# Transposing DMAs for tokens and attention output, a reordered head and new planner constants in a two-layer attention and FFN kernel

## The chip, the cores and the metric

The kernel runs on one core of one Trainium2 chip. The metric is the device time of one execution in microseconds; a time of a kernel is the median over several runs. A core has five engines that each work through their own instruction stream in order: TensorE (PE in the profile, PEld its weight loads), VectorE (DVE), ScalarE (ACT), GpSimd (POOL) and SyncE (SP, which issues DMAs). They wait for each other through semaphores.

## The reference

Two equal layers over 2048 tokens of width 512, in bfloat16, with 32 heads of 16 channels and an FFN of width 1792:

```python
def _A_ref(x, wqkv, wo):
    qkv = (x @ wqkv).reshape(B, S, 3, H, Dh).transpose(2, 0, 3, 1, 4)
    q, k, v = qkv[0], qkv[1], qkv[2]
    scores = jnp.einsum("bhqd,bhkd->bhqk", q, k) * (Dh ** -0.5)
    p = softmax(scores)
    o = jnp.einsum("bhqk,bhkd->bhqd", p, v)
    return o.transpose(0, 2, 1, 3).reshape(B, S, D) @ wo

def _B_ref(x, w_gate, w_up, w_down):
    return (gelu(x @ w_gate) * (x @ w_up)) @ w_down

for layer in range(2):
    x = x + _A_ref(layernorm(x), A_wqkv, A_wo)
    x = x + _B_ref(layernorm(x), B_w_gate, B_w_up, B_w_down)
```

Both layers use the same weights. The score matrices have 2 x 32 x 2048 x 2048 elements, and each needs a row maximum and an exponential.

## The kernel before, in words

**Data.** All weights, the keys (`KT`), the values (`VP`) and the residual stream (`X`, float32, 16 tiles of 128 tokens) stay in SBUF. `XNT` holds the normalised tokens with channels on the partitions, as projections need them; `ATT` holds the attention output of a block of up to 512 queries, tokens on the partitions, and `ATTT` two transposed tiles of it for the output projection.

**Work units.** A unit is a block of queries (512, and at the end of the second layer 256 and 128) times a group of four heads; there are 80 units. Each goes through two phases. In phase 1 PE multiplies queries and keys into PSUM (L1724) and DVE reduces each 128x512 tile to row maxima (L1742, one or two tiles an instruction). The negated maxima, transposed into `MT`, are moved by four small DMAs into spare rows of `QT` (L1127), so that phase 2's matmul, which computes the scores transposed (L1594), subtracts them. ACT takes the exponential from PSUM to `SCR` (L1570, one or two tiles an instruction), and PE multiplies that with the values and a column of ones (L1618) into bank 7. ACT copies the result to `ACCS`, POOL takes the reciprocal of the sum (L1186) and multiplies into `ATT` (L1191).

**Folds.** DVE's share can be shifted to ACT: PE multiplies queries with the difference of two key blocks (`KD`, L1543), ACT writes its Relu to `SCR` (L1550), and one DVE instruction (L1737) adds that to the other block's scores and takes the maximum of both. Without a fold two tiles are reduced, with it one instruction does for two.

**Background work.** Between the score tiles the kernel puts projections, output projections, the FFN, layer norms and transposes, each a generator ("chain") that yields when it needs an engine. `ln_to_xnt` normalises up to four tiles into two buffers `XN` (on POOL for most, DVE and ACT at the head) and transposes each: `transpose_tile` issues four 128x128 PE transposes against an identity (L866) into a PSUM bank, and `evac` copies the bank to `XNT` or `ATTT` on ACT (L720) or DVE (L718). `outproj` does the same from `ATT` to `ATTT`, one tile ahead of the matmul with `WO` (L703).

**What sets the order.** All streams are written out on the host before launch. A planner keeps a clock for each engine, with a fixed duration for each kind of instruction, and at each step emits what fits; `_Sched` turns data dependences into semaphore waits. So what the chip runs is a fixed order for each engine. 21 constants (how far phase 1 may run ahead, when to fold, in which pieces background work goes, and so on) change every 16 pairs of score tiles, by the table `PLAN`. PE also runs filler matmuls on a zero weight (L1766) to keep its clock up.

**Head.** SP loads the tokens and weights. DVE makes the statistics of tiles 0 to 7 (L730, L732, L733), POOL the power of -1/2 (L735), DVE the normalised tile (L742); ACT does the same for tiles 8 to 15 (L838, L845). The first four tiles feed the projections of `QT` and `KT` (L703, cast to `SG`, then moved by DMA at L1010 and L940). ACT first copies the pattern of ones and zeros into `KT` for two head groups (L566).

Of the kernel before, what the change touches and what calls it, by code (L numbers as in the profile page):

```python
# [8 lines left out]
ALU = mybir.AluOpType  # L9
# [5 lines left out]
LN_EPS = 1e-5  # L15
# [138 lines left out]
]  # L154


# [1853 lines left out]
```

## Time and profile before

| | |
|---|---|
| median of 3 runs | 2487.87 us (2487.69 to 2489.23) |
| profiled execution, its own time | 2489.29 us |
| span of its instructions | 2487.6 us |
| busy PE, DVE, ACT, POOL | 2416.8, 2388.4, 2353.1, 811.5 us |
| granted TensorE clock | 0.999 |
| DMA moved | 25.67 MB, mean 10 GB/s |

Busy time is the union of an engine's instructions. A group row gives line, engine, operation, output and input, count, then busy us and mean ns of one, then the engine's idle time just before such instructions and what ended it. A stretch row gives for each engine the busy us within the stretch. Times are from the span's start.

### The profile page before, as it was taken

The page shows a single profiled execution, that of the slowest core. Times are in us where ns is not written, and L with a number is a line of the kernel's source. Part 1 is how long each engine was busy: PE and PEld are TensorE (multiplying, and loading weights), DVE is VectorE, ACT ScalarE, POOL GpSimd, SP SyncE. Part 2 cuts the span into 40 slices and gives each one's busy share as a digit, 9 for nine tenths or more (in the row PEclk, how much of TensorE's full clock was granted, in tenths as well). Part 3 has the DMA queues.
Part 4 walks back from the last instruction along what each step waited for, and adds up shares of the span by engine and source line. Part 5 has one row for each costly group of instructions (what it writes and reads, how often), then busy time and mean ns, then how long its engine had stood idle before and what let it go on. Part 6 is the DMA issues. An engine that isn't in the chain of part 4 may idle for free.

```text
span 2487.6 us, 69334 instructions
## 1 busy us (share of the span) xinstructions
PE 2416.8 (97%) x30182; PEld 1152.2 (46%) x30182; DVE 2388.4 (96%) x3168; ACT 2353.1 (95%) x3394; POOL 811.5 (33%) x1298
## 2 busy tenths in 40 slices
PE   8999999999999999999999999999999999999999
PEld 3444445434454444344433445434444344544655
DVE  8999999999999999999998999999999999999993
ACT  7999999999999999899988999999999999989987
POOL 4112125234442353421224041543116321244420
PEclk9999999999999999999999999999999999999999
DMA  3110000000000000000000000000000000000000
GB/s 94 48 57 6 4 9 2 6 2 2 6 2 6 2 2 6 2 10 11 11 10 1 9 15 4 6 2 6 11 2 6 2 8 6 3 3 11 4 4 10
DMA packets 28913, 25.67 MB, mean 10 GB/s; under 512 B 10944, under 2 KB 27584, under 8 KB 28608
## 3 DMA queue, kind: packets, MB, share of 16 engines
q1 hardware_dynamic: 28608, 21.24, 3.3%
q8 instruction: 236, 3.87, 0.6%
q14 instruction: 69, 0.57, 0.1%
HBM read 10.22 MB, written 2.10 MB: 5 GB/s over the span
## 4 chain that ended last, share of the span: by engine, by line
PE 45%; DVE 31%; ACT 23%; issue 1%; ACTq 0%
DVE PM L1742 29%; ACT SCR L1570 21%; PE PS L1724 14%; PE PS L703 12%; PE PS L1618 10%; PE PS L1594 4%; PE PS L1766 3%; DVE SCR L1737 2%; ACT SCR L1550 1%; PE PS L866 1%; PE PS L1543 0%; ACT SG L720 0%; ACT XNT L720 0%; ACT L1286 0%; ACT ACCS L1176 0%
## 5 line engine op out<-in xcount | busy, mean ns | idle before, releaser
L1742 DVE TENSOR_REDUCE PM<-PS 128x1 f32<-128x512 f32 (+1 forms) x2527 | 2203.8, 934 | 47.4 <-PE PS L1594 19.5
L1570 ACT ACTIVATE SCR<-PS 128x1024 bf16<-128x1024 f32 (+1 forms) x2652 | 2015.4, 871 | 46.9 <-PE PS L1594 32.9
L1724 PE MATMUL PS<-KT,QT 32*128 32x512 bf16 x3908 | 1021.0, 385 | 38.0 <-DVE PM L1742 21.1
L1594 PE MATMUL PS<-QT,KT 32*128 32x512 bf16 (+2 forms) x5120 | 929.5, 340 | 3.1 <-ACT SCR L1570 2.2
L1618 PE MATMUL PS<-VP,SCR 128*128 128x51 bf16 (+1 forms) x16384 | 802.5, 187 | 9.8 <-ACT SCR L1570 6.1
L1618 PEld LDWEIGHTS PS<-VP,SCR 128*128 128x128 bf16 x16384 | 571.3, 96 | 471.8 <-issue 398.2
L1724 PEld LDWEIGHTS PS<-KT,QT 32*128 32x128 bf16 x3908 | 243.8, 91 | 543.8 <-DVE PM L1742 317.3
L1766 PE MATMUL PS<-WV,ZER 128*128 128x240 bf16 x2198 | 408.8, 266 | 5.5 <-ACT SCR L1570 3.6
L1186 POOL TENSOR_TENSOR RL<-ACCS,CM 128x16 f32<-128x16 f32 (+2 forms) x71 | 182.4, 2569 | 449.5 <-ACT ACCS L1176 449.0
L1594 PEld LDWEIGHTS PS<-QT,KT 32*128 32x128 bf16 x5120 | 250.5, 91 | 71.2 <-ACT SCR L1570 41.5
L1766 PEld LDWEIGHTS PS<-WV,ZER 128*128 128x128 bf16 x2198 | 165.2, 96 | 56.1 <-issue 39.7
L1083 POOL TENSOR_TENSOR PM<-PM 128x16 f32<-128x16 f32 (+3 forms) x142 | 32.6, 230 | 426.4 <-DVE PM L1742 410.4
L1304 POOL TENSOR_TENSOR HT<-HT,AO 128x512 bf16<-128x512 bf16 x96 | 111.2, 1162 | 173.9 <-ACT AO L1302 173.8
L1341 POOL TENSOR_TENSOR KD<-KT 128x512 bf16<-128x512 bf16 x80 | 92.3, 1155 | 154.3 <-PE PS L1543 154.3
L703 PE MATMUL PS<-WD,HT 128*128 128x512 bf16 x448 | 131.3, 381 | 0.0
L703 PE MATMUL PS<-XNT,WU 128*128 128x512 bf16 (+2 forms) x504 | 131.1, 357 | 0.1
L1550 ACT ACTIVATE SCR<-PS 128x512 bf16<-128x512 f32 (+1 forms) x134 | 105.8, 790 | 22.3 <-PE PS L1543 20.7
L1737 DVE CUSTOM_DVE_ANT_0 SCR<-PS,SCR 128x512 bf16<-128x512 f32 x188 | 121.9, 686 | 3.2 <-PE PS L1594 0.7
L703 PE MATMUL PS<-XNT,WG 128*128 128x512 bf16 (+2 forms) x504 | 121.3, 358 | 1.7 <-ACT HT L1286 1.7
L1206 POOL TENSOR_TENSOR X<-X,AO 128x512 f32<-128x512 f32 x45 | 57.0, 1268 | 184.3 <-ACT AO L1204 184.3
L1286 ACT ACTIVATE HT<-PS 128x512 bf16<-128x512 f32 (+2 forms) x126 | 68.4, 550 | 31.6 <-PE PS L703 31.1
L1191 POOL TENSOR_TENSOR ATT<-ACCS,RL 128x256 bf16<-128x256 f32 (+2 forms) x78 | 41.8, 536 | 67.1 <-DVE RL L1184 61.5
(118 smaller groups left out, 1112.5 us busy)
## 6 DMA issues: line engine op xcount, KB each, us to landing
KT<-SG SPq DMA_DIRECT2D x64, 64.0 KB
QT<-MT SPq DMA_DIRECT2D x244, 1.0 KB
QT<-SG SPq DMA_DIRECT2D x56, 64.0 KB
out_dram<-AO SPq DMA_DIRECT2D x16, 128.0 KB, 1.7
WG<-in_B_w_gate_dram SPq DMA_DIRECT2D x4, 448.0 KB, 4.8
WU<-in_B_w_up_dram SPq DMA_DIRECT2D x4, 448.0 KB, 5.1
WD<-in_B_w_down_dram SPq DMA_DIRECT2D x4, 384.0 KB, 4.7
QT<-MT SPq DMA_DIRECT2D x68, 0.2 KB
```

The costliest lines, as they stand in the source:

```text
L703: ins = e.matmul(out_ap, lhsT=l, rhs=r_, start=(i == 0), stop=(i == n - 1))
L1186: emit("pool", lambda e: e.tensor_tensor(RL[:, s, 0:4 * nq], lsum, AP(CM1, 0, [[1, 128], [0, 4 * nq]]), op=ALU.pow), r=[("ACCS", s), ("CM1 ...
L1304: emit("pool", lambda e, ft=ft, o=o: e.tensor_tensor(HT[:, ft, c0:c0 + n], HT[:, ft, c0:c0 + n], AO[:, o, 0:n], op=ALU.mult), r=[("AO", o) ...
L1341: emit("pool", lambda e: e.tensor_tensor(KD[:, s, :], KT[:, g, ka * 512:(ka + 1) * 512], KT[:, g, kb * 512:(kb + 1) * 512], op=ALU.subtrac ...
L1550: emit("act", lambda e: e.activation(PT[:, s0:s0 + cnt, :], PS[:, bk:bk + cnt, :], ACTF.Relu), r=bks, w=[("PT", s0 + d) for d in range(cnt ...
L1570: emit("act", lambda e: e.activation(dst, src, ACTF.Exp, scale=DH ** -0.5), r=[BK[bk + i] for i in range(cnt)], w=[("PT", i) for i in slot ...
L1594: ins = e.matmul(bank(bk)[:, i * n:(i + 1) * n], lhsT=KT[32 * j:32 * j + 32, g, kt * 128:(kt + 1) * 128], rhs=QT[32 * j:32 * j + 32, s, 0: ...
L1618: ins = e.matmul(acc, lhsT=PT[:, slot, i * n + qt * 128:i * n + (qt + 1) * 128], rhs=AP(VP, (kt * H + 4 * g + j) * 17, [[NTT * H * 17, 128 ...
L1724: ins = e.matmul(bank(b), lhsT=QT[32 * j:32 * j + 32, s, qt * 128:(qt + 1) * 128], rhs=KT[32 * j:32 * j + 32, g, kb * 512:(kb + 1) * 512], ...
L1737: emit("dve", lambda e, i=i, b=b, sl=sl: e.tensor_tensor_reduce(PT[:, sl, :], bank(b), PT[:, sl, :], 1.0, -3.0e38, ALU.add, ALU.max, po[:, ...
L1742: emit("dve", lambda e: e.tensor_reduce(po, PS[:, bs[0]:bs[0] + cnt, :], axis=AX.X, op=ALU.max), r=bks, w=[("PM", sm) + h[1:] for h in hs] ...
L1766: return e.matmul(PS[:, b, NACC:512], lhsT=ZER[:, :], rhs=WV[:, 0, 0:512 - NACC], start=(b != 7), stop=(b != 7), skip_group_check=True)
```

## The change

1. *Transposing DMAs.* Where a layer norm's tile goes to `XNT` and where a tile of `ATT` goes to `ATTT`, SP issues one `dma_start_transpose` of 128x512 instead of four PE transposes and an evacuation. Kept on PE: the first layer's tokens at the head, the last tiles of the first layer (its last attention block, its last FFN group and the tokens of the next layer that come from it), and the end of the second layer. The planner reckons 2.0 us of SP and 1.6 + 0.7 us until the tile has landed. There are four new DMA groups, alternating by tile; a DMA of a group waits for the one before it.
2. *Head.* Planner durations for the loads, for POOL's `KT` fills and a start at 0.6 us are set anew; loads no longer queue behind each other in its clock. ACT fills one block of `KT` for two groups, POOL the other three. Tile 3's mean and variance come from ACT (`ln_a3`); tiles 2 and 3 are normalised into `ATT` so that they need not wait for the transposes of 0 and 1; the evacuations of tiles 0 to 2 and the first query projection go to ACT. The 14 filler matmuls before the first score are dropped.
3. *Constants.* 109 of the 132 rows of `PLAN` differ, so the whole order of the streams does.

```diff
+        if grp is not None and self.groups[grp] and o.idx:
+            need((grp, o.idx - 1))
...
-        ... LM1=0, N0=14):
+        ... LM1=0, T0=0.6, A3=1, DTX=2, DTA=2, T_TP=0.7, T_TPI=2.0, VL=0):
...
+        tp_groups = ["tx0", "tx1", "ty0", "ty1"] if DTX or DTA else []
...
-                clk[eng] = start + T_DMA * nd
+                clk[eng] = start + (T_TPI if grp[0] == "t" else T_DMA * nd)
                 done = max(clk["dma"], clk[eng] + 1.6) + dur
-                clk["dma"] = done - 1.6
+                clk["dma"] = done - carry
...
-            emit(eng, lambda e: e.dma_start(dst, src), r=r, w=w, grp=grp, dur=mb * 5.0)
+            emit(eng, lambda e: e.dma_start(dst, src), r=r, w=w, grp=grp, dur=mb * 2.9, carry=0.0)
...
         for g in range(NFE):
-            kt_fill(g, "act")
+            kt_fill(g, "act", 0, 1 if A3 else NKB)
...
+        def ln_a3(tt):
+            c = [ACCS[:, 1, 40 + j:41 + j] for j in range(5)]
+            yield ("act", [XSK[tt]], [("X", tt)])
+            emit("act", lambda e: e.activation(X[:, tt, :], XS[tt], ACTF.Copy, accum_out=c[0]), ...)
+            yield ("pool", [("A3",)], [("A3",)])
+            emit("pool", lambda e: e.tensor_scalar(c[1], c[0], -1.0 / D, None, op0=ALU.mult), ...)
+            yield ("act", [("A3",)], [("AH", 3)])
+            emit("act", lambda e: e.activation(ATT[:, 3, :], XS[tt], ACTF.Square, bias=c[1], accum_out=c[2]), ...)
+            yield ("pool", [("A3",)], [("A3",)])
+            emit("pool", lambda e: e.tensor_scalar(c[3], c[2], 1.0 / D, LN_EPS, op0=ALU.mult, op1=ALU.add), ...)
+            emit("pool", lambda e: e.tensor_tensor(c[4], c[3], CM05[:, 0:1], op=ALU.pow), ...)
...
+        def dma_tile(src, rkeys, dst, wkeys, grp):
+            emit("sp", lambda e: e.dma_start_transpose(dst, src), r=list(rkeys), w=list(wkeys), grp=grp, dur=T_TP)
...
             for i, tt in enumerate(tts):
+                xs, sk = xn_slot(i, A3 and tag == ("in", 0) and tts[0] == 0)
                 yield ("cond", lambda i=i: at["xn"] >= i)
+                if DTX and tag != ("in", 0) and not fast and (DTX == 1 or tag not in (("mid", 0), ("in", 1)) or tts[-1] * 128 + 128 < S):
+                    yield ("sp", [sk], [("XNT", tt)])
+                    dma_tile(xs, [sk], XNT[:, :, tt * 128:(tt + 1) * 128], [("XNT", tt)], "tx%d" % (i % 2))
+                    ...
+                    continue
...
+            te = "sp" if DTA and not lastb and (DTA == 1 or la or t0 + n < S) else "pe"
             def tr(qt):
+                if te == "sp":
+                    dma_tile(ATT[:, qt, :], ak, ATTT[:, qt % 2, :, :], [("ATTT", qt % 2)], "ty%d" % (qt % 2))
+                else:
+                    transpose_tile(...)
...
-            if not pos["g"]:
-                for _ in range(N0):
-                    sch.op("pe", warm_fn(7), r=[("ZER",), ("WV",)], w=[BK[7]])
```

More of the change, by code (lines that the diff above doesn't have):

```diff
@@ L387, in _build @@
             sch.add_dma_group(g, serial=True)
-        dma_groups += out_groups + move_groups
+        tp_groups = ["tx0", "tx1", "ty0", "ty1"] if DTX or DTA else []
+        for g in tp_groups:
+            sch.add_dma_group(g, serial=True)
+        dma_groups += out_groups + move_groups + tp_groups
         for o in range(2):
@@ L396, in _build @@
         clk = {e: 0.0 for e in ("pe", "act", "dve", "pool", "sp", "dma")}
+        for e in clk:
+            clk[e] = T0
         rgf = [0.0] * 4
@@ L567, in kt_fill @@
                 KT[:, g, b0 * 512:b1 * 512].rearrange("p (a b) -> p a b", b=512), AP(HT, 0, [[NFT * ft_tok, 128], [0, b1 - b0], [1, 512]])),
-                r=[("HT", 0)], w=[("KT", g, b) for b in range(b0, b1)], dur=0.05 + 0.438 * (b1 - b0) if eng == "act" else 0.74 * (b1 - b0))
-            if b1 == NKB:
-                filled.add(g)
+                r=[("HT", 0)], w=[("KT", g, b) for b in range(b0, b1)], dur=0.05 + 0.438 * (b1 - b0) if eng == "act" else 0.08 + 0.48 * (b1 - b0))
+            filled.update((g, b) for b in range(b0, b1))
         N_FILL = NFA
         for g in range(NFE):
-            kt_fill(g, "act")
+            kt_fill(g, "act", 0, 1 if A3 else NKB)
         xn_late = [0]
         def fills_act():
+            if A3:
+                yield ("cond", lambda: xnt_rec.get(3) == ("in", 0))
+                for b in range(1, NKB):
+                    for g in range(NFE):
+                        yield ("pool", [("HT", 0)], [("KT", g, b)])
+                        kt_fill(g, "pool", b, b + 1)
             yield ("cond", lambda: kt_rec.get((0, NKB - 1)) == 0)
@@ L590, in fills @@
             for tt in range(8):
+                if A3 and tt == 3:
+                    continue
                 yield ("pool", [XSK[tt]], [("X", tt)])
@@ L722, in _build, with xn_slot, ln_fast @@
         ln_cnt = {"n": 0}
-        def ln_fast(tts, x_of, ready, at, dx=0.6):
+        sch.add_alias(("A3",), ("ACCS", 1))
+        def ln_a3(tt):
+            c = [ACCS[:, 1, 40 + j:41 + j] for j in range(5)]
+            yield ("act", [XSK[tt]], [("X", tt)])
+            emit("act", lambda e: e.activation(X[:, tt, :], XS[tt], ACTF.Copy, accum_out=c[0]),
+                 r=[XSK[tt]], w=[("X", tt), ("A3",)], dur=0.62)
+            yield ("pool", [("A3",)], [("A3",)])
+            emit("pool", lambda e: e.tensor_scalar(c[1], c[0], -1.0 / D, None, op0=ALU.mult), r=[("A3",)], w=[("A3",)], dur=0.24)
+            yield ("act", [("A3",)], [("AH", 3)])
+            emit("act", lambda e: e.activation(ATT[:, 3, :], XS[tt], ACTF.Square, bias=c[1], accum_out=c[2]),
+                 r=[XSK[tt], ("A3",)], w=[("AH", 3), ("A3",)], dur=0.7)
+            yield ("pool", [("A3",)], [("A3",)])
+            emit("pool", lambda e: e.tensor_scalar(c[3], c[2], 1.0 / D, LN_EPS, op0=ALU.mult, op1=ALU.add), r=[("A3",)], w=[("A3",)], dur=0.24)
+            emit("pool", lambda e: e.tensor_tensor(c[4], c[3], CM05[:, 0:1], op=ALU.pow), r=[("A3",), ("CM05",)], w=[("A3",)], dur=0.59)
+            a3["done"] = True
+        a3 = {}
+        def xn_slot(i, head):
+            return (ATT[:, i - 2, :], ("AH", i - 2)) if head and i >= 2 else (XN[:, i % 2, :], ("XN", i % 2))
+        def ln_fast(tts, x_of, ready, at, dx=0.6, late=None):
+            head = late is not None
             for i in range(len(tts) + 1):
-                if i < len(tts):
+                if i < len(tts) and tts[i] != late:
                     xa, xk = x_of(tts[i])
@@ L739, in ln_fast @@
                     xa, xk = x_of(tts[k])
-                    yield ("cond", lambda k=k: at["tr"] > k - 2)
-                    yield ("dve", [xk, ("LNR", k)], [("XN", k % 2)])
-                    emit("dve", lambda e, k=k, xa=xa: e.tensor_scalar(
-                        XN[:, k % 2, :], xa, MV[:, k, 0:1], LNS[:, 1, k:k + 1], op0=ALU.subtract, op1=ALU.mult),
-                        r=[xk, ("MV", k), ("LNR", k)], w=[("XN", k % 2)], dur=dx)
+                    xs, sk = xn_slot(k, head)
+                    yield ("cond", lambda k=k: head or at["tr"] > k - 2)
+                    if tts[k] == late:
+                        yield ("cond", lambda: "done" in a3)
+                        yield ("dve", [xk, ("A3",)], [sk])
+                        emit("dve", lambda e, xa=xa, xs=xs: e.tensor_scalar(
+                            xs, xa, ACCS[:, 1, 41:42], ACCS[:, 1, 44:45], op0=ALU.add, op1=ALU.mult),
+                            r=[xk, ("A3",)], w=[sk], dur=dx)
+                        at["xn"] = k
+                        continue
+                    yield ("dve", [xk, ("LNR", k)], [sk])
+                    emit("dve", lambda e, k=k, xa=xa, xs=xs: e.tensor_scalar(
+                        xs, xa, MV[:, k, 0:1], LNS[:, 1, k:k + 1], op0=ALU.subtract, op1=ALU.mult),
+                        r=[xk, ("MV", k), ("LNR", k)], w=[sk], dur=dx)
                     at["xn"] = k
@@ L892, in ln_to_xnt @@
             if tag == ("in", 0):
-                add(ln_fast(tts, x_of, ready, at, 0.3), due)
+                if A3 and tts[0] == 0:
+                    add(ln_a3(3), due)
+                add(ln_fast(tts, x_of, ready, at, 0.3, 3 if A3 and tts[0] == 0 else None), due)
             else:
@@ L930, in kproj @@
                 yield ("cond", lambda: last_u in p2_done)
-            yield ("cond", lambda: 2 * c in filled and 2 * c + 1 in filled)
+            yield ("cond", lambda: (2 * c, b) in filled and (2 * c + 1, b) in filled)
             yield ("cond", lambda: all(xnt_rec.get(4 * b + i) == ("in", la) for i in range(4)))
@@ L946, in vproj @@
         def vproj(la, tt):
+            if not la and VL:
+                yield ("cond", lambda: kt_rec.get((0, NKB - 1)) == 0)
             if la:
@@ L998, in qproj @@
             yield ("cond", lambda: all(xnt_rec.get(tt) == ("in", la) for tt in tts))
-            s = yield from proj(WQ, "WQ", g // 2, t0, n, tts)
+            s = yield from proj(WQ, "WQ", g // 2, t0, n, tts, "act" if A3 and u == 0 else None)
             for i in range(2):
@@ L1217, in outproj @@
             nq = n // 128
+            te = "sp" if DTA and not lastb and (DTA == 1 or la or t0 + n < S) else "pe"
             def tr(qt):
[L1219 to L1220 removed]
+                if te == "sp":
+                    dma_tile(ATT[:, qt, :], ak, ATTT[:, qt % 2, :, :], [("ATTT", qt % 2)], "ty%d" % (qt % 2))
+                else:
+                    transpose_tile(lambda ck: ATT[:, qt, ck * 128:(ck + 1) * 128], ak, ATTT[:, qt % 2, :, :],
+                                   [("ATTT", qt % 2)])
                 if qt == nq - 1:
                     att_free["bi"] = bi
[L1224 removed]
+            yield (te, ak, [("ATTT", 0)])
             tr(0)
@@ L1229, in outproj @@
                 if qt + 1 < nq:
-                    yield ("pe", ak, [("ATTT", 1 - s)])
+                    yield (te, ak, [("ATTT", 1 - s)])
                     tr(qt + 1)
```

32 lines of the change are left out of this document (17 added, 15 removed), and 210 rows, old and new, of the table PLAN.

## The prediction

> **What bounds the kernel now.** I read the page first: engine shares, the 40 slices, the chain that ended last.
>
> ```profile
> span 2487.6 us, 69334 instructions
> PE 2416.8 (97%) x30182; PEld 1152.2 (46%) x30182; DVE 2388.4 (96%) x3168; ACT 2353.1 (95%) x3394; POOL 811.5 (33%) x1298
> ...
> DVE  8999999999999999999998999999999999999993
> ACT  7999999999999999899988999999999999989987
> ...
> DVE PM L1742 29%; ACT SCR L1570 21%; PE PS L1724 14%; PE PS L703 12%; PE PS L1618 10%; PE PS L1594 4%; PE PS L1766 3%; DVE SCR L1737 2%; ACT SCR L1550 1%; PE PS L866 1%; PE PS L1543 0%; ACT SG L720 0%; ACT XNT L720 0%; ACT L1286 0%; ACT ACCS L1176 0%
> ```
>
> DVE (row maxima) and ACT (exponentials) are both full nearly everywhere; PE's 97% includes filler matmuls (L1766), so it is not the limit by itself. The transposes and their evacuations have about 1% of the chain (PE L866), so they count through the engine time that they take, not as links. Then the stretch view, for where DVE still idles:
>
> ```profile
> 450.00:475.00 25.00, 24.43 (x340) 12.63 (x340) 24.82 (x35) 24.96 (x29) 5.85 (x12) 1.00 0.01 2
> ...
> 1350.00:1375.00 25.00, 24.68 (x262) 10.51 (x260) 21.20 (x30) 21.10 (x31) 10.28 (x17) 1.00 0.01 1
> ...
> 2425.00:2450.00 25.00, 24.95 (x462) 15.43 (x457) 12.27 (x25) 24.54 (x36) 0.88 (x3) 1.00 0.01 3
> 2450.00:2475.00 25.00, 24.58 (x366) 14.14 (x365) 6.24 (x15) 19.49 (x26) 1.62 (x5) 1.00 0.05 17
> ```
>
> The columns after the length are busy PE, PEld, DVE, ACT, POOL. In mid layer DVE has 24.8 of 25 us, ACT as much. At the layer seam both drop (21.2). In the tail DVE is done and ACT, with PE, sets the end. So a change is worth what it takes off DVE up to its last reduction, plus what it takes off ACT and PE behind that, plus the head.
>
> **DVE's work.** Each count below is the difference between the built instruction streams of the two kernels; each duration is of this trace.
>
> ```profile
> L1742 DVE TENSOR_REDUCE PM<-PS 128x2 f32<-128x1024 f32 x1193 | 1443.6, 1217 | 30.2 <-PE PS L1594 14.0 <-PE PS L1724 6.0 <-PE PS L1543 0.4
> L1742 DVE TENSOR_REDUCE PM<-PS 128x1 f32<-128x512 f32 x1334 | 895.9, 681 | 17.2 <-PE PS L1594 5.5 <-PE PS L1724 5.3
> L1737 DVE CUSTOM_DVE_ANT_0 SCR<-PS,SCR 128x512 bf16<-128x512 f32 x188 | 121.9, 686 | 3.2 <-PE PS L1594 0.7 <-PE PS L1724 0.6
> L1737 DVE DVE_READ_ACCUMULATOR2_ANT PM<- 128x1 f32 x188 | 15.6, 83 | 0.0
> L1296 DVE TENSOR_TENSOR HT<-PS,HT 128x512 bf16<-128x512 f32 x2 | 1.4, 686 | 0.0
> ```
>
> The new constants fold 14 more score tiles (a fold lets ACT take a Relu of a difference, so that one DVE pass serves two tiles). Folds: +14 x (0.686 + 0.083) = +10.8 us. Double reductions fall by 8: -8 x 1.217 = -9.7. Single ones fall by 12: -12 x 0.681 = -8.2. Five more products go into HT on DVE: +5 x 0.686 = +3.4. Two additions into X and a handful of small head forms leave it: about -3.8 (estimate, at 0.2 to 0.7 us each). Sum: **-7.5 us**. DVE did almost no transposition evacuations, so the DMA transposes give it nothing directly; its gain comes through the folds that ACT's freed time pays for.
>
> **ACT's work.**
>
> ```profile
> L1570 ACT ACTIVATE SCR<-PS 128x1024 bf16<-128x1024 f32 x1444 | 1382.5, 1074 | 31.1 <-PE PS L1594 23.4 <-PE PS L1724 0.7
> L1570 ACT ACTIVATE SCR<-PS 128x512 bf16<-128x512 f32 x1208 | 668.4, 629 | 15.7 <-PE PS L1594 9.5
> L1302 ACT ACTIVATE AO<-PS 128x512 f32<-128x512 f32 x96 | 59.2, 617 | 1.9 <-POOL HT L1304 1.1 <-PE PS L703 0.3
> ...
> L1550 ACT ACTIVATE SCR<-PS 128x1024 bf16<-128x1024 f32 x54 | 57.7, 1069 | 2.4 <-PE PS L1543 2.4
> L1550 ACT ACTIVATE SCR<-PS 128x512 bf16<-128x512 f32 x80 | 48.1, 601 | 19.9 <-PE PS L1543 18.3 <-PE PS L1724 1.1
> L720 ACT ACTIVATE XNT<-PS 128x512 bf16<-128x512 bf16 x61 | 38.6, 644 | 3.6 <-PE PS L866 3.4
> ...
> L720 ACT ACTIVATE ATTT<-PS 128x512 bf16<-128x512 bf16 x31 | 20.0, 648 | 2.1 <-PE PS L866 2.1
> ```
>
> The stream has 39 DMA transposes into XNT and 27 into ATTT; ACT loses 39 x 0.644 + 26 x 0.648 = -42.0 us of evacuations. It gains the folds' Relus, 4 x 0.601 + 5 x 1.069 = +7.7, and pays for a split that the new constants choose: 74 double exponentials become 148 single ones, 148 x 0.629 - 74 x 1.074 = +13.6. Three fewer AO copies: -1.9. KT fills given to POOL against the third tile's statistics taken over: about 0. Sum: **-22.6 us**, three times DVE's.
>
> **PE's work.**
>
> ```profile
> L1766 PE MATMUL PS<-WV,ZER 128*128 128x240 bf16 x2198 | 408.8, 266 | 5.5 <-ACT SCR L1570 3.6 <-ACT ACCS L1176 1.0 <-DVE PM L1742 0.3
> ...
> L866 PE MATMUL PS<-IDN,XN 128*128 128x128 bf16 x224 | 22.8, 226 | 9.2 <-DVE XN L742 9.2
> L866 PE MATMUL PS<-IDN,ATT 128*128 128x128 bf16 x160 | 15.3, 220 | 0.2 <-ACT AO L1204 0.2
> ```
>
> 264 of the 384 transposes go: 264 x (22.8 + 15.3)/384 = -26 us. 86 more fillers come: 86 x 408.8/2198 = +16. PE is relieved by 10 us that were not the limit; I count nothing for it.
>
> **Head.**
>
> ```profile
> 10.13 0.41 DVE L742 TENSOR_SCALAR XN<-SCR,MV,LNS 128x512 bf16<-128x512 bf16 x1
> 12.19 1.91 PE L703 MATMUL PS<-XNT,WQ 128*128 128x512 bf16 x4
> 17.05 0.69 DVE L718 CAST SG<-PS 128x512 bf16<-128x512 f32 x1 [0.89 <-PE PS L703]
> 20.96 0.38 PE L1724 MATMUL PS<-KT,QT 32*128 32x512 bf16 x1
> 21.39 0.69 DVE L1742 TENSOR_REDUCE PM<-PS 128x1 f32<-128x512 f32 x1 [0.97 <-PE PS L1724]
> ```
>
> The first projection waits for four normalised tiles; the fourth is written at 10.13. ACT now makes that tile's mean and square, which takes a statistics chain out of DVE's line and drops the six fillers that stood ahead of the projection. But ACT's two passes, its first evacuation and three POOL steps still follow each other, so I give it 1.0 us, between 0 and 2. The 14 fillers before the first score at 20.96 cost nothing now (the score waits for KT's move, issued after the cast at 17.05), so dropping them gives nothing. Head: **-1.0 us**.
>
> **Tail.**
>
> ```profile
> 2430.18 1.79 DVE L1742 TENSOR_REDUCE PM<-PS 128x2 f32<-128x1024 f32 x2
> ```
>
> Behind the last reduction (2431.97) the span runs 55.6 us more. Behind the last score matmul the old stream holds 304 quarter-tile phase-2 matmuls, the new one 276: 7 tiles of exponentials fewer, 7 x 1.074/2 = -3.8 us of ACT. Four more FFN matmuls stand there, at most +1.5 us of PE by the row of 0.38 us a score matmul. I take **-2.5**, between -3.8 and 0.
>
> **The DMAs.** What the trace does not show is a transposing DMA. Nearest rows, the last number being issue to landing in us, and the queue's waits:
>
> ```profile
> out_dram<-AO SPq DMA_DIRECT2D x16, 128.0 KB, 1.7
> ...
> HT<-in_A_x_dram SPq DMA_DIRECT2D x2, 512.0 KB, 8.6
> ```
>
> ```profile
> SPq L1127 <- DVE MT L1087: 1228.1, 54, 53.0
> ```
>
> A tile is 128 KB, so from release to landing I bound it by 1.7 and 8.6 us, and take 4: above the row of the same bytes, since it is cut finer. Does that hide? In the FFN a block is transposed between its last out-projection matmul and its first gate matmul, and the stream holds 20 to 91 phase-1 score tiles there. For third and fourth out-projection tiles 10 to 15 score tiles (0.61 us each by the double reduction) lie between the buffer's release and its reader: 6.1 to 9.2 us of cover. The least covered are 12 readers: the first out-projection tile of eight blocks and four V projections at the seam, placed where the planner expects the tile, 4.3 us after its source (its constants 2.0 + 1.6 + 0.7). If a tile is later, PE stands in order and all scores behind it; DVE and ACT run on for about a banked pair each, 1.2 us. Queued behind a transpose on SP are the next units' MT-to-QT moves, but SP waits 1228.1/54 = 23 us for each of those, and phase 2 runs 58 tiles or more behind, 35 us. POOL now waits for DMAs before reusing XN; it is 33% busy. So at 4 us the price is zero.
>
> The Trainium skill speaks against the swap: VectorE: DVE Perf Modes, in The three transpose paths, gives 1309 ns for a 128x128 block by DMA against 390 ns on TensorE, and its rules prefer TensorE where PSUM will do. By that figure a tile of four blocks would take 4 x 1309 ns = 5.2 us and, with half a microsecond to issue it, end at 5.7 (an estimate): 12 x 0.2 = 2 us of stalls, and a sum of -9. No trace here shows a transposing DMA yet.
>
> **Sum.** -7.5 - 1.0 - 2.5 = -11.0 us. The profiled execution took 2489.29 us around its span of 2487.6; it lies 1.4 us above the runs' median of 2487.87. 2487.87 - 11.0 = **2476.9, so 2477**.
>
> **Rivals.**
>
> *Both engines cash in (2465).* ACT gives 15 us more than DVE. If that also shortens DVE's waits (47.4 us stand before its reductions in the rows above, mostly after PE phase-2 matmuls that share PE's order with ACT's banks), a quarter of them is another -12. For: both engines are saturated in mid layer. Against: freed ACT time was spent on splitting exponentials, a sign of slack there.
>
> *It turns into idle time (2487).* New constants also move the seam, where DVE lost 3.8 us in 1350 to 1375 alone; 10 us more idling over the two seam stretches and the mid layers eats the sum. The planner's own durations are not the chip's, so a fresh plan may fit worse.
>
> *Slower: late tiles (2489 to 2514).* If a tile lands later than 4.3 + 1.2 = 5.5 us after its source, each of the 12 least covered readers stalls by the excess. The sum is gone at 12 x (L - 5.5) = 11, L = 6.4 us; at the upper bound of 8.6 the price is 12 x 3.1 = +37, so 2514. For: the upper row, and four tiles in a row on one queue. Against: that row moves four times the bytes.
>
> *Not done as told:* excluded, the stream holds the 66 transposes.
>
> **Numbers.** 0.2%, 5 us, is about what a measurement of this kernel can tell from no change. Chances: forecast 0.57, both cash in 0.17 (together faster, 0.74); idle time 0.12 (same); late tiles 0.14 (slower). The forecast's own bounds (head 0 to -2, tail 0 to -3.8) give 2475 to 2480. The range runs from 2462, a little under the first rival, to 2493, where L is 6.8: below lie some 0.06, above some 0.11.
>
> **What would show it.** Right: DVE busy near 2381 and ACT near 2330, the L720 XNT and ATTT groups at 22 and 5; first reduction near 20.4; last reduction to end near 53 us; PE waits on the transposes' queue near zero. Wrong: PE matmuls on ATTT or XNT led by DMA waits of over a microsecond; DVE idle above 107 us, above all in 1000 to 1425; a landing above 6.4 us.

## The result, and the profile after

The changed kernel takes 2481.66 us (median of 9 runs, 2480.65 to 2481.82), the kernel before 2488.09 us beside it (9 runs, 2487.44 to 2490.97). The ratio is 0.997, with an interval of 0.996 to 0.998: faster by 6.4 us. The profiled execution took 2481.77 us, around a span of 2480.0; its span is 7.6 us shorter than the one of before, whose profiled execution lay 1.2 us above its median while this one lies at its own.

From the page of the changed kernel, span, engine shares, two rows of the slices and the chain that ended last:

```profile
span 2480.0 us, 69071 instructions
PE 2409.1 (97%) x30004; PEld 1147.4 (46%) x30004; DVE 2382.1 (96%) x3173; ACT 2331.1 (94%) x3415; POOL 810.2 (33%) x1311
...
DVE  8999999999999999999998999999999999999993
ACT  7999998999989999899989999989999999978987
...
DVE PM L1806 31%; ACT SCR L1637 17%; PE PS L1791 16%; PE PS L717 13%; PE PS L1685 10%; PE PS L1661 4%; PE PS L1830 4%; DVE SCR L1801 1%; ACT SCR L1617 1%; PE PS L1610 0%; PE PS L914 0%; ACT AO L1266 0%; ACT ACCS L1238 0%; ACT L1637 0%; DVE ST L769 0%
```

ACT lost 22.0 us of work, DVE 6.3, PE 7.7. On the chain ACT's exponentials went from 21% to 17%, DVE's maxima from 29% to 31%, and the PE transposes (L914 now) from 1% to nothing. The groups (reductions L1806, folds L1801 with their Relus L1617, exponentials L1637, evacuations L736, fillers L1830):

```profile
L1806 DVE TENSOR_REDUCE PM<-PS 128x2 f32<-128x1024 f32 x1185 | 1433.6, 1218 | 35.2 <-PE PS L1661 18.1 <-PE PS L1791 5.9 <-PE PS L1610 0.2
L1637 ACT ACTIVATE SCR<-PS 128x1024 bf16<-128x1024 f32 x1370 | 1297.9, 1074 | 20.6 <-PE PS L1661 14.7
L1806 DVE TENSOR_REDUCE PM<-PS 128x1 f32<-128x512 f32 x1322 | 887.5, 681 | 12.3 <-PE PS L1661 7.1 <-PE PS L1791 1.3
L1637 ACT ACTIVATE SCR<-PS 128x512 bf16<-128x512 f32 x1356 | 726.6, 619 | 25.3 <-PE PS L1661 17.5
...
L1801 DVE CUSTOM_DVE_ANT_0 SCR<-PS,SCR 128x512 bf16<-128x512 f32 x202 | 130.1, 686 | 3.2 <-PE PS L1661 1.2 <-PE PS L1791 0.6 <-PE PS L1610 0.2
...
L736 ACT ACTIVATE XNT<-PS 128x512 bf16<-128x512 bf16 x19 | 11.4, 619 | 4.0 <-PE PS L914 4.0
...
L736 ACT ACTIVATE ATTT<-PS 128x512 bf16<-128x512 bf16 x5 | 3.0, 608 | 2.1 <-PE PS L914 2.1
```

The transposing DMAs, in the list of DMA issues (last number: median us from issue to landing), and in the waits (us in total, times, longest) the only engine that ever waited for one:

```profile
XNT<-XN SPq DMA_TRANSPOSE x39, 2.4
ATTT<-ATT SPq DMA_TRANSPOSE x27, 2.5
```

```profile
POOL XN L838 <- DMA XNT<-XN: 9.8, 3, 4.1
```

PE has no wait on them at all. Where the 7.6 us of span went is seen by cutting both spans at the start of the first reduction and at the end of the last. The columns after the length are busy PE, PEld, DVE, ACT, POOL; before first, then after:

```profile
0.00:21.39 21.39, 12.62 (x70) 7.07 (x71) 14.71 (x41) 15.76 (x33) 7.67 (x26) 1.00 0.62 190
21.39:2431.97 2410.58, 2351.91 (x29284) 1112.49 (x29282) 2358.04 (x3085) 2296.57 (x3301) 801.61 (x1266) 1.00 0.03 9
2431.97:2487.60 55.63, 52.27 (x831) 32.65 (x829) 15.60 (x44) 40.72 (x63) 2.21 (x7) 1.00 0.04 11
```

```profile
0.00:20.16 20.16, 11.27 (x57) 5.32 (x58) 13.67 (x37) 13.27 (x32) 10.02 (x31) 1.00 0.65 202
20.16:2426.86 2406.70, 2347.76 (x29181) 1110.78 (x29178) 2352.45 (x3094) 2279.84 (x3323) 797.99 (x1274) 1.00 0.05 12
2426.86:2480.00 53.14, 50.08 (x771) 31.32 (x769) 15.94 (x45) 37.95 (x62) 2.19 (x7) 1.00 0.04 12
```

Head -1.2, middle -3.9, tail -2.5. In the middle DVE has 5.6 us less work (2358.04 to 2352.45), but it idles 1.7 us more (2410.58 - 2358.04 = 52.5 before, 54.3 after). That extra idling has a place, 2200 to 2400 us, the second layer's small blocks; before, then after:

```profile
1000.00:1450.00 450.00, 437.41 (x5140) 198.30 (x5140) 425.34 (x563) 418.47 (x595) 127.67 (x181) 1.00 0.04 8
...
2200.00:2400.00 200.00, 196.73 (x3040) 105.89 (x3038) 196.06 (x249) 185.53 (x284) 85.39 (x170) 1.00 0.03 6
```

```profile
1000.00:1450.00 450.00, 441.50 (x5297) 202.17 (x5296) 428.81 (x555) 428.34 (x645) 139.22 (x187) 1.00 0.04 9
...
2200.00:2400.00 200.00, 193.19 (x3176) 108.35 (x3175) 191.33 (x244) 190.66 (x306) 78.88 (x161) 1.00 0.04 10
```

DVE's idle time there goes from 3.9 to 8.7 us, while ACT has 5 us more to do. Between 1000 and 1450 us it falls by 3.5.

Not all of that is the change. In the profiled execution of before, TensorE's granted clock (the column after POOL) fell once, to half for 3.4 us from 1409 us on. e10 below has the order of before behind the head, and in its profiled execution the clock stays at 1.0. The same stretch, before and in e10:

```profile
1400.00:1425.00 25.00, 24.09 (x319) 12.35 (x316) 23.27 (x35) 23.52 (x30) 2.42 (x5) 0.93 0.01 2
```

```profile
1400.00:1425.00 25.00, 24.12 (x339) 12.43 (x337) 24.48 (x37) 24.66 (x31) 2.41 (x5) 1.00 0.01 2
```

The reductions behind it come 1.3 us earlier in e10, beyond the lead that e10 had ahead of it. So about 1.3 us of the middle's 3.9 is this fall, about as much as that execution stood above its median (1.2).

### The profile page after: what moved, and what is told of

Its sections match the earlier page's. It is cut to its first block, busy times and chain, and to the rows that moved or that the text cites. A ratio compares the mean times of both kernels' runs of the same rounds, so it can differ in the third digit from the quotient of the medians.

```text
span 2480.0 us, 69071 instructions
## 1 busy us (share of the span) xinstructions
PE 2409.1 (97%) x30004; PEld 1147.4 (46%) x30004; DVE 2382.1 (96%) x3173; ACT 2331.1 (94%) x3415; POOL 810.2 (33%) x1311
## 4 chain that ended last, share of the span: by engine, by line
PE 47%; DVE 33%; ACT 19%; issue 1%; POOL 0%; ACTq 0%
DVE PM L1806 31%; ACT SCR L1637 17%; PE PS L1791 16%; PE PS L717 13%; PE PS L1685 10%; PE PS L1661 4%; PE PS L1830 4%; DVE SCR L1801 1%; ACT SCR L1617 1%; PE PS L1610 0%; PE PS L914 0%; ACT AO L1266 0%; ACT ACCS L1238 0%; ACT L1637 0%; DVE ST L769 0%
## 5 line engine op out<-in xcount | busy, mean ns | idle before, releaser
L1806 DVE TENSOR_REDUCE PM<-PS 128x1 f32<-128x512 f32 (+1 forms) x2507 | 2189.9, 935 | 47.6 <-PE PS L1661 25.1
L1637 ACT ACTIVATE SCR<-PS 128x512 bf16<-128x512 f32 (+1 forms) x2726 | 2005.9, 848 | 45.9 <-PE PS L1661 32.2
L1661 PE MATMUL PS<-QT,KT 32*128 32x512 bf16 (+2 forms) x5120 | 919.3, 340 | 2.6 <-ACT SCR L1637 1.7
L1685 PE MATMUL PS<-VP,SCR 128*128 128x51 bf16 (+1 forms) x16384 | 802.9, 187 | 10.1 <-ACT SCR L1637 5.3
L1830 PE MATMUL PS<-WV,ZER 128*128 128x240 bf16 x2284 | 419.9, 265 | 3.9 <-ACT ACCS L1238 1.9
L1661 PEld LDWEIGHTS PS<-QT,KT 32*128 32x128 bf16 x5120 | 247.6, 91 | 73.9 <-ACT SCR L1637 44.3
L1830 PEld LDWEIGHTS PS<-WV,ZER 128*128 128x128 bf16 x2284 | 170.0, 96 | 70.0 <-issue 57.3
L1145 POOL TENSOR_TENSOR PM<-PM 128x16 f32<-128x16 f32 (+3 forms) x142 | 32.4, 228 | 425.0 <-DVE PM L1806 410.7
L1371 POOL TENSOR_TENSOR HT<-HT,AO 128x512 bf16<-128x512 bf16 x91 | 105.4, 1161 | 174.0 <-ACT AO L1369 174.0
L1617 ACT ACTIVATE SCR<-PS 128x512 bf16<-128x512 f32 (+1 forms) x143 | 112.1, 787 | 26.3 <-PE PS L1610 25.3
L1801 DVE CUSTOM_DVE_ANT_0 SCR<-PS,SCR 128x512 bf16<-128x512 f32 x202 | 130.1, 686 | 3.2 <-PE PS L1661 1.2
L1353 ACT ACTIVATE HT<-PS 128x512 bf16<-128x512 f32 (+2 forms) x126 | 68.5, 550 | 43.1 <-PE PS L717 42.3
L717 PEld LDWEIGHTS PS<-XNT,WG 128*128 128x128 bf16 x504 | 37.6, 97 | 57.8 <-issue 33.2
```

The lines of the kernel that those rows point to most:

```text
L717: ins = e.matmul(out_ap, lhsT=l, rhs=r_, start=(i == 0), stop=(i == n - 1))
L1371: emit("pool", lambda e, ft=ft, o=o: e.tensor_tensor(HT[:, ft, c0:c0 + n], HT[:, ft, c0:c0 + n], AO[:, o, 0:n], op=ALU.mult), r=[("AO", o) ...
L1617: emit("act", lambda e: e.activation(PT[:, s0:s0 + cnt, :], PS[:, bk:bk + cnt, :], ACTF.Relu), r=bks, w=[("PT", s0 + d) for d in range(cnt ...
L1637: emit("act", lambda e: e.activation(dst, src, ACTF.Exp, scale=DH ** -0.5), r=[BK[bk + i] for i in range(cnt)], w=[("PT", i) for i in slot ...
L1661: ins = e.matmul(bank(bk)[:, i * n:(i + 1) * n], lhsT=KT[32 * j:32 * j + 32, g, kt * 128:(kt + 1) * 128], rhs=QT[32 * j:32 * j + 32, s, 0: ...
L1685: ins = e.matmul(acc, lhsT=PT[:, slot, i * n + qt * 128:i * n + (qt + 1) * 128], rhs=AP(VP, (kt * H + 4 * g + j) * 17, [[NTT * H * 17, 128 ...
```

## The experiments

My theory: DVE's work bounds; the DMAs are hidden and are worth the ACT time that they free, which pays for folds; head and tail give the rest. Rivals: ACT's time counts directly; the new constants alone give the gain; the DMAs' lateness costs something already. Four kinds of kernels tell these apart: the order of a kernel is kept and one cost is added or removed in it (e1 to e4, e9, e11, e12); a part of the change is undone and the rest planned anew (e5 to e7); a stretch of the constants is undone (e8); and one detail of the head (e10). The time before was 2488.1 to 2488.2 us beside all of them; "after" is 2481.66.

**Are the transposing DMAs free where they stand?** e2 makes 64 of the 66 nearly nothing.

```diff
-            emit("sp", lambda e: e.dma_start_transpose(dst, src), ...)
+            emit("sp", lambda e: e.dma_start(dst[0:1, 0, 0:32], src[0:1, 0:32]), ...)
```

> The order of the changed kernel is kept; 64 of the 66 transposing DMAs (all but the first into each ATTT buffer) are replaced by a plain DMA of 32 elements, so those tiles are left out. It shows what the transposing DMAs cost where they stand. My theory (hidden, price 0): 2480 to 2483, no wait of PE changes. The late-tile rival in a mild form (the 12 least covered readers lose up to 1 us each): 2470 to 2478.

Measured: 2481.76 us (2481.06 to 2482.39), the same as after. At their real 2.4 us the DMAs cost nothing. That settles the mild form of the late-tile rival.

**How much later could they be?** e12 does each DMA twice, e3 three times, one behind the other. A repeat waits until the one before has landed, and SP waits with it.

```diff
         def dma_tile(src, rkeys, dst, wkeys, grp):
+            for z in range(1):     # e3: range(2)
+                sch.op("sp", lambda e: e.dma_start_transpose(dst, src), r=list(rkeys), w=list(wkeys), grp="tz%d" % z)
             emit("sp", lambda e: e.dma_start_transpose(dst, src), ...)
```

> The order of the changed kernel is kept; each transposing DMA is done three times in a row into the same tile, each after the one before has landed, so that a tile is there some 2.4 x 3 = 7.2 us or more after its source instead of 2.4. By the forecast's price, 12 readers x (7.2 - 5.5) = +20 us: about 2502. If the cover is larger than I took it to be: 2480 to 2485. If also the moves behind the transposes on SP's queue come late: above 2510.

> As the triple one, but each transposing DMA is done twice in a row into the same tile, so that a tile is there some 2 x 2.4 = 4.9 us after its source: between the 4 us that the forecast took and the 5.7 that follows from the figure of the Trainium skill. By the forecast's price (nothing up to 5.5 us, 12 readers beyond it): 2481 to 2483. If every bit of lateness beyond the real 2.4 us costs as in the triple kernel (193 us for 4.9 us more): 2481.7 + 193 x 2.5/4.9 = 2580. If the cover reaches somewhere between: 2490 to 2550.

Measured: e3 2674.67 us (2672.86 to 2679.2), e12 2533.87 us (2530.77 to 2541.22): 193 and 52 us over after, where the forecast's price gave 20 and nothing. Waits on the DMAs in e12, with SP's own behind them, then in e3:

```profile
POOL XN L838 <- DMA XNT<-XN: 28.3, 9, 6.4
PE PS L717 <- DMA XNT<-XN: 16.2, 5, 4.4
...
SPq L923 <- DMA XNT<-XN: 55.3, 39, 2.8
SPq L923 <- DMA ATTT<-ATT: 42.0, 27, 3.2
```

```profile
PE PS L717 <- DMA XNT<-XN: 70.6, 7, 16.2
POOL XN L838 <- DMA XNT<-XN: 56.3, 11, 12.6
PE PS L717 <- DMA ATTT<-ATT: 42.5, 21, 4.0
```

The tiles are later than the expectations took them to be. From the end of the write of `XN` to the last landing, the 39 `XNT` tiles take 3.1 us in the median and 7.6 at most in the changed kernel, 7.8 and 12.7 in e12, 12.5 and 17.8 in e3, where the expectations have 4.9 for e12 and 7.2 for e3. SP's queue makes the difference: what stands behind a repeat stands until SP has seen the landing before it. Around e3's longest wait, SP first, then POOL's writes of `XN`:

```profile
414.09 3.90 SPq L922 DMA_TRANSPOSE XNT<-XN  x2
419.18 1.19 SPq L923 DMA_TRANSPOSE XNT<-XN  x1
420.41 3.67 SPq L922 DMA_TRANSPOSE XNT<-XN  x2
425.38 1.19 SPq L923 DMA_TRANSPOSE XNT<-XN  x1
426.62 2.73 SPq L1191 DMA_DIRECT2D QT<-MT  x4
429.39 3.62 SPq L922 DMA_TRANSPOSE XNT<-XN  x2
```

```profile
414.08 0.77 POOL L838 TENSOR_SCALAR XN<-X,LNS 128x512 bf16<-128x512 f32 x1
...
421.70 0.77 POOL L838 TENSOR_SCALAR XN<-X,LNS 128x512 bf16<-128x512 f32 x1 [2.94 <-DMA XNT<-XN]
...
428.95 0.77 POOL L838 TENSOR_SCALAR XN<-X,LNS 128x512 bf16<-128x512 f32 x1 [6.45 <-DMA XNT<-XN]
```

The second tile is written at 414.85, but SP comes to it at 420.41, behind the first tile's three DMAs. The third is written at 422.47; SP comes to it at 429.39, behind the second tile's three and four moves of `MT`. The four tiles of a block also share two `XN` buffers, so POOL waits as well, but the third tile is ready 6.9 us before SP is. So e12 and e3 price late tiles and a held queue together. What a DMA would cost that only lands later, and holds SP no longer, they do not show.

The other part of the price is the clock. These are stretches of e3, with PE's wait for `XNT` between 340 and 460 us behind them:

```profile
350.00:375.00 25.00, 19.27 (x170) 7.50 (x173) 15.37 (x17) 16.03 (x30) 3.63 (x3) 0.71 0.29 54
...
425.00:450.00 25.00, 10.74 (x47) 2.87 (x49) 9.56 (x15) 6.27 (x11) 4.56 (x12) 0.64 0.24 43
```

```profile
PE PS L717 <- DMA XNT<-XN: 14.0, 1, 14.0
```

Where PE waits, its granted clock falls to 0.64 to 0.71, and with it the matmuls run slower: a 32x512 score matmul of e3 takes 603 ns (median) where the clock is at half and 385 elsewhere. Over the whole span e3 has 0.948, e12 0.988, after 1.0. The traces have no clock but 1.0 and 0.5, so that is some 276 us at half in e3 and 62 in e12. So a wait of PE costs more than itself. The Trainium skill says so in TensorE: Matmul & The Clock Gate, under HAM oscillation: PE idle gaps of more than some 3.4 us bring the clock down. The trace agrees in kind (a wait of 14.0 us, the clock at 0.64 in its stretch); the threshold was not measured.

**What is an engine's time worth at a given order?** e4 adds an idle reduction on DVE, e11 two idle copies on ACT, beside each transposing DMA; e9 takes the kernel before and shortens 64 evacuations.

```diff
+            sch.op("dve", lambda e: e.tensor_reduce(KBIAS[:, 1:2], AP(IDN, ...), axis=AX.XY, op=ALU.max), ...)        # e4
+            for _ in range(2):                                                                                       # e11
+                sch.op("act", lambda e: e.activation(IDN[:], IDN[:], ACTF.Copy), w=[("IDN",)])
+            if cut and (w[0][0] != "ATTT" or w[0] in sch.last_w):                                                    # e9, in evac
+                dst, src = dst[:, 0:1, 0:16], src[:, 0:1, 0:16]
```

> The order of the changed kernel is kept; beside each of the 66 transposing DMAs DVE runs one more reduction over 512 elements of SBUF whose result nobody uses, some 0.55 us each, 36 us together. If DVE's work is the bound at the places where these stand, the time grows by 30 to 36 us, to about 2514. If DVE and the others share the bound and slack swallows part of it: 2490 to 2505. If DVE is not the bound: under 2487.

> The changed kernel with its order kept; beside each of the 66 transposing DMAs ACT runs two more copies of a 128x128 tile in place, some 0.6 us together, 40 us in all, which nobody waits for. If ACT's time is not the bound (the forecast's step): 2482 to 2490. If ACT is as much a bound as DVE, where 44.4 us more work cost 47.2 us: about 2520. If part of it is swallowed by slack: 2495 to 2512.

> The kernel before with its order kept; of the evacuations of those tiles that the change gives to DMAs, 64 write only 16 columns instead of 512 (their transposed tiles are left out otherwise), which frees some 62 x 0.42 = 26 us of ACT and nothing of DVE, and adds no latency. The forecast's step (ACT's time is worth nothing by itself, only through the folds that it pays for): 2486 to 2489. The rival that both engines cash in (waits of DVE shorten as well): 2476 to 2483. If ACT's time counts in full: 2462.

The engine rows of the three pages, e4, e11, e9 (some traces lack a few matmul records, so PE's figures are not compared):

```profile
PE 2408.8 (95%) x29800; PEld 1149.7 (45%) x30004; DVE 2419.5 (96%) x3239; ACT 2337.6 (92%) x3415; POOL 810.1 (32%) x1311
```

```profile
PE 2407.1 (96%) x29800; PEld 1151.9 (46%) x30004; DVE 2388.3 (95%) x3173; ACT 2360.7 (94%) x3547; POOL 810.2 (32%) x1311
```

```profile
PE 2388.2 (96%) x29979; PEld 1149.9 (46%) x30182; DVE 2386.7 (96%) x3168; ACT 2335.7 (94%) x3394; POOL 809.4 (33%) x1298
```

e4: 2528.88 us (2526.37 to 2532.43), 47.2 over after for 37.4 us more of busy DVE; the 66 reductions last 44.4 us, part of it overlapped. e11: 2514.08 us (2511.35 to 2514.95), 32.4 over after for 29.6 us more of busy ACT; the 132 copies last 42.3 us. So counting ACT's time at nothing is wrong for additions.

But part of both prices is the clock. Its mean is 0.987 to 0.989 in e4's runs and 0.995 to 0.997 in e11's, and the profiled executions have 61 and 27 us at half clock. Both kernels run the same 2507 reductions of scores in the same order, and how much later each ends than in the changed kernel gives the delay stretch by stretch, here cut between the groups of transposes. Stretches in which the clock did not fall lost 6.1 us for 10.1 us of added reductions in e4, and 11.6 us for 19.6 us of added copies in e11: 0.6 us for each added, on either engine. Those in which it fell lost 44.3 us for 34.3, and 22.9 for 22.7. The full price of additions is thus an average over places with and without a fall of the clock; that the added work brings the falls is likely, since the changed kernel has none, but how was not tested.

e9: 2485.16 us (2484.81 to 2486.19), ratio 0.9988 (0.9979 to 0.9997): 3.0 us for 17.4 us less of busy ACT (I had expected 26). Work taken off ACT alone gives a sixth of itself. Beside the transposes both engines are a bound, so that adding to either shows; relieving ACT alone gives little, and relieving DVE alone was not tried. The 149 us for which ACT stands idle in the changed kernel are no reserve: in e11 they are 152.5. e9's time lies between what the forecast's step and the rival expected, nearer to the step.

**The swap alone, at the changed kernel's order.** e1 puts the transposes back on PE and ACT, each where its source is ready.

```diff
-            emit("sp", lambda e: e.dma_start_transpose(dst, src), ...)
+            real_op("pe", pe_fn, r=list(rkeys) + [("IDN",)], w=[BK[b]])          # four transposes into a bank
+            real_op("act", lambda e: e.activation(dst, bankbf(b)[...], ACTF.Copy), r=[BK[b]], w=list(wkeys))
```

> The order of the changed kernel is kept on every engine, and each of the 66 transposing DMAs is put back as four TensorE transposes and one evacuation on ACT, at the place where its source is ready. ACT gets 66 x 0.64 = 42 us back, PE 26 us; DVE has the same work as in the changed kernel. My theory (the DMAs' worth is the ACT time, and DVE's work is what bounds): ACT's busy time near 2373, and the time between 2487 and 2507, since ACT has only some 150 us idle and stands next to DVE in the mid layers. If ACT's time counts in full: 2481.7 + 42 = 2524. If the swap is worth nothing by itself and only the new order counts: 2480 to 2484.

```profile
PE 2442.3 (95%) x30063; PEld 1171.9 (45%) x30268; DVE 2390.9 (93%) x3173; ACT 2373.1 (92%) x3481; POOL 811.7 (31%) x1311
```

Measured: 2572.0 us (2569.52 to 2580.93), 90 over after, more than any theory gave. ACT's busy time is the 2373 that I expected, so the size of the work was right and its price was not. In the profiled execution, the slowest of the four, DVE's idle time rises from 97.9 to 188.3 us (2579.2 - 2390.9), and the clock is 0.982, which is 92 us at half. An order made for free transposes has little room for them; how much of the 90 us is room and how much is clock was not separated. It does not say what the swap is worth in an order made for PE transposes; e9 gives the ACT part of that, 3 us.

**Parts undone, the rest planned anew.** e5 has `DTX=0, DTA=0`, e6 the old table `PLAN`, e7 `A3=0`.

> The changed kernel with its new constants and head, but the 66 tiles transposed on TensorE and evacuated by ACT or DVE as before, and the order planned anew for that. Its stream has 168 folds instead of 202, 58 more single reductions, 5 more double ones and 3 more products into HT on DVE. My theory (the DMAs free ACT time, which pays for folds, and DVE's work bounds): DVE's work grows by 58 x 0.68 + 5 x 1.22 - 34 x 0.77 = 19 us, so about 2500, and more if the constants also fit the new order badly (up to 2520). If the DMAs are worth nothing and the constants bring the gain: 2480 to 2485. If the swap matters by ACT's own time alone: 2481.7 + 42 = 2524.

> The changed kernel, DMAs and head kept, with the constants of before. Its stream has 160 folds instead of 202, 44 more double reductions and 4 fewer single ones, and 37 us less of ACT's work. If DVE's work is the bound: + 44 x 1.22 - 4 x 0.68 - 42 x 0.77 = 18.6 us, about 2500. If DMAs and head bring the gain and the constants only shuffle: 2478 to 2486. If constants and order belong together and a foreign set costs idle time as well: above 2505.

> The changed kernel with its constants and DMAs, but the head of before (third tile's statistics on DVE, all fills as before); the rest is planned anew and has 200 folds, 10 more single and 3 fewer double reductions. My theory: first reduction 1.2 us later, and 1.6 us more of DVE's work: 2483 to 2486. If the new head costs or saves nothing: 2481 to 2483. If the small shift upsets the order behind it: above 2488.

| kernel | us, runs | over after | busy DVE | idle DVE |
|---|---|---|---|---|
| after | 2481.66 (2480.65 to 2481.82) | | 2382.1 | 97.9 |
| e5, PE transposes | 2545.24 (2545.02 to 2549.95) | 63.6 | 2417.4 | 125.9 |
| e6, old constants | 2533.86 (2533.05 to 2535.96) | 52.2 | 2405.3 | 128.9 |
| e7, old head | 2490.08 (2489.3 to 2490.59) | 8.4 | 2386.1 | 101.7 |

e5 and e6 are slower than before, e7 is as before (ratio 1.0006, 0.9998 to 1.0015). Busy DVE is 35.3 of the 63.6 us in e5 and 23.2 of the 52.2 in e6; 28.0 and 31.0 us are new idling. I took 19 from the counts for each. The sum of all durations on DVE grows by 28.6 in e5 and by 12.2 in e6; the rest of the busy time is neighbours that overlap less. So the third reading of e6's expectation holds, and e5 went beyond all of its own. Neither the DMAs nor the constants give the gain by themselves. But this is no price of either part, since each order wants constants of its own; what the DMAs would give with the old order searched anew wasn't tried.

e7 was the miss among them. First scores and first reductions (start, us, engine, line) after, then in e7:

```profile
11.24 1.86 PE L717 MATMUL PS<-XNT,WQ 128*128 128x512 bf16 x4 [0.56 <-issue]
...
19.27 0.39 PE L1791 MATMUL PS<-KT,QT 32*128 32x512 bf16 x3
...
20.16 1.22 DVE L1806 TENSOR_REDUCE PM<-PS 128x2 f32<-128x1024 f32 x1
```

```profile
11.66 1.86 PE L717 MATMUL PS<-XNT,WQ 128*128 128x512 bf16 x4 [0.56 <-issue]
...
18.81 0.39 PE L1791 MATMUL PS<-KT,QT 32*128 32x512 bf16 x3
```

With the old statistics the first projection is 0.4 us later, but the first score is not: 18.81, and in the other kernels with the new head it stands anywhere from 17.94 (e11) to 19.31 (e6). Such a lead is not lost at once. In e2, whose order is that of after, the first reduction comes 0.8 us earlier, and so does the one at 2125 us; the lead ends at 2161.8, where the granted clock falls for 3.4 us in that execution. e7's head is 0.8 us shorter than that of after. Its loss lies between the first reduction and the last: 8.6 us, of which 2.5 are busy DVE and 6.1 idling. That is the third reading, a shift that upsets the order behind it.

**The end.** e8 takes the last 17 rows of `PLAN` from before.

> The changed kernel with the last 17 of the 132 rows of constants (from about 2200 us on) taken from before; the order up to there is the same. DVE's idle time between 2200 and 2400 us was 3.9 us before and 8.7 after the change. If the new rows there cause it: some 4 to 5 us less, 2476 to 2478, with the tail as long as in the changed kernel. If the rows shorten the tail and this idle time is their price: the tail back at 55.6 and the time 2482 to 2485. If only the order as a whole counts: anything from 2478 to 2490.

```profile
2200.00:2400.00 200.00, 190.76 (x3092) 107.56 (x3113) 194.43 (x250) 187.00 (x282) 84.58 (x165) 1.00 0.05 10
```

Measured: 2482.49 us (2481.71 to 2482.87), within a microsecond of after, and the same span. DVE idles 5.6 us there instead of 8.7, and the last reduction ends 8.2 us earlier:

```profile
2416.82 1.81 DVE L1806 TENSOR_REDUCE PM<-PS 128x2 f32<-128x1024 f32 x2
```

From 2418.63 to the end at 2480.0 it is 61.4 us instead of 53.1. About 1.2 of the 8.2 us stem from an earlier start of that execution. What the old end rows save before the last reduction they give back behind it. So 3.1 us less idling of DVE at 2200 to 2400 bring nothing by themselves.

**The 14 fillers.** e10 drops them from the kernel before (`N0=0`).

> The kernel before without the 14 filler matmuls that stand ahead of the first score; all else and its order as before. The forecast's step (they cost nothing, since the score waits for K's move): 2487.5 to 2488.7, with the first score at 20.96 as before. If they delay the projections behind them: the first score 1 to 2 us earlier, 2485.5 to 2487. If PE's clock needs them: 2489 or more.

```profile
19.94 0.37 PE L1724 MATMUL PS<-KT,QT 32*128 32x512 bf16 x1 [0.23 <-DMA KT<-SG]
```

The first score moves from 20.96 to 19.94, and only there waits for K's move: before, it waited behind the fillers, not for that move. The first reduction comes 0.9 us earlier; of that 0.3 is left at 116 us and 0.2 at 1375. The time does not move for it: five of the eleven runs take 2487.66 to 2489.17 us at a mean clock of 0.999 to 1.0. The other six take 2493.68 to 2496.91, at 0.996 to 0.997, and so the median is 2493.68. Without the fillers the clock falls in some executions and costs 6 to 9 us; the changed kernel drops them too and shows no such run among its nine.

## Why the prediction was right, and where not

The forecast was 2477, faster; it is faster, by 6.4 instead of 11.0 us. By its own steps:

*DVE's work, -7.5.* Busy DVE fell by 6.3, 5.6 of it in the middle. The counts held. The sizing was 1.2 us too large: the two kinds of reductions became 0.6 and 0.3 ns longer in the mean, some 1.1 us over 2507 of them, and the small forms gave 3.5 instead of 3.8. Neighbours on DVE overlap, so that all durations add up to 2596.56 us before and 2590.45 after, well over the busy time; but the overlap is 208 us in both, and the sum falls by 6.1, as the busy time does by 6.3. 0.7 us net of the saving lies in the head and the tail, which the sum counted again.

*Idle time, 0.* It rose by 1.7 in the middle. With the DVE term's 1.9 that is missing in the middle, less 0.2 more in the head, this is the difference between -11.0 and the -7.6 of the spans; the last 1.2 is the fall of the clock in the profiled execution of before. Against e10's execution, whose middle has 51.7 us of idle DVE (2410.17 - 2358.45) at a clock of 1.0, the rise is 2.5. That idling would stay as it was is a term that the sum put at nothing without a reason.

*ACT's work, -22.6, counted only through the folds.* It fell by 22.0. e9 supports not counting it: 17.4 us less of ACT gave 3.0. But the reason was not slack on ACT (e11); more likely DVE stays a bound when ACT is relieved, which no run tests by itself. So the rival that both engines cash in fails, at a sixth instead of its size.

*PE, -10, counted nothing.* It fell by 7.7. That it counts nothing is not general: in e3 PE's waits cost more than their length.

*Head, -1.0.* The first reduction came 1.2 us earlier, as forecast, but the step is not shown: e7 has its first reduction earlier still (19.37) without ACT's help, and executions with the new head differ by more than a microsecond there (18.82 in e11, 20.20 in e6). Whether the 1.2 us reach the end is open: e2 keeps a lead of 0.8 us to 2125 us, e10 loses most of one of 0.9 in the order of before. The sentence that the first score waits for K's move was wrong (e10).

*Tail, -2.5.* It is 2.5, from 55.6 to 53.1. That it counts as a term of its own was luck: e8 has the tail 8.2 us longer at the same span.

*The DMAs, price nothing.* True (e2). I took 4 us from release to landing; from the issue it is 2.4. But what I left out is SP's queue in front of the issue: I counted its 23 us of waiting for each unit's moves as room, while four tiles and such moves come close together. So 9 of the 39 `XNT` tiles land over 5.5 us after their source in the changed kernel, up to 7.6, and still cost nothing: the edge of 5.5 us does not hold for these. Whether any of the 12 tight readers hangs on one of them is open. In e12 and e3 the queue makes the tiles 7.8 and 12.5 us late in the median. The rival's rule, 12 x (L - 5.5), gives 28 and 84 us for that; 52 and 193 were measured, part of it through the clock. So the slower rival has the right direction and is too cheap, and it did not happen.

The Trainium skill, VectorE: DVE Perf Modes, The three transpose paths, gives 1309 ns for one 128x128 block, from which I estimated 5.7 us for a tile and a loss of 2 us. The measurement decides: 2.4 us for four blocks. What 5.7 us would have cost no run shows, since e12 also holds SP.

*It turns into idle time.* Partly: 4.8 us of new idling at 2200 to 2400, against 3.5 saved at 1000 to 1450, 1.2 of them by the clock. e8 has 3.1 us less of the new idling and is no faster.

What stays open is how the 6.4 us divide between DMAs, head and constants.

## What to carry to other kernels

Where two engines are full at once, a saving on one may be worth little until the order is made anew (here a sixth, for ACT), while anything added to either shows: 0.6 of its length here where TensorE's clock held, and its full length or more where it fell. The cover of a transfer is counted from its source to its landing, with the issuing queue in between: before moving a step to a DMA, ask what stands before it in that queue, and who refills the source buffer. An idle time that the sum leaves as it was is a term too. And two profiled executions can differ by a fall of the clock that has nothing to do with the change; look at the clock stretch by stretch before comparing them.

## What the runs showed of the hardware that was not expected

Two rows on the transposing DMAs of the changed kernel (ns of the issue, least, median and most; then us to the landing of all 66):

```profile
L921 SPq DMA_TRANSPOSE XNT<-XN x39: 1188/1192/1785, 401.4 to 2398.5; - x39
...
DMA to landing us min/median/max: 2.4/2.4/4.4
```

A tile of 128x512 bfloat16, 128 KB, holds SP's queue for 1.19 us and has landed after 2.4.

TensorE's granted clock is 1.0 throughout in the profiled execution of after. In single stretches of 25 us it falls to 0.57 in e3, to 0.73 in e1 and e11, to 0.74 in e4 and e12. It also falls where nothing was added: to 0.93 once in before, which cost 1.3 us, and once in e2. In e10 the loss of 14 small matmuls in the first 21 us was enough, in six of eleven executions, to lower the mean by 0.003 to 0.004 and lose 6 to 9 us; where in the span it fell in these is not on record.
